# Uneven key blocks, 128-token rows, and keys and queries transposed as float32r words, in an attention and channel-mixing kernel

## The chip, the cores and the metric

The kernel runs on one core of one Trainium2 chip, in one launch. The metric is the device time of an execution in microseconds (us), the median of several; every time below is of the hardware profiler or of these executions.

## The reference, cut to what matters

```python
# q, k, v: (4, 12, 448, 64) float32
scores = (1.0 / np.sqrt(64)) * np.matmul(q, k.transpose(0, 1, 3, 2))
scores = np.where(mask, -1000000000.0, scores)       # causal, 448 x 448
scores = scores - np.max(scores, axis=-1, keepdims=True)
attn = np.exp(scores)
attn = attn / (np.sum(attn, axis=-1, keepdims=True) + 1e-09)
attn_out = np.matmul(attn, v)                        # -> x: (4, 448, 768)
xt = x.transpose(0, 2, 1)                            # token mixing
u = x + (np.maximum(xt @ w_tok1, 0.0) @ w_tok2).transpose(0, 2, 1)
x = u + np.maximum(u @ w_ch1, 0.0) @ w_ch2           # channel mixing
x_prev = shift_by_one_token(x)
xk = mu_k * x + (1.0 - mu_k) * x_prev
xr = mu_r * x + (1.0 - mu_r) * x_prev
k = np.maximum(xk @ w_k, 0.0)
out = 1.0 / (1.0 + np.exp(-(xr @ w_r))) * (k * k @ w_v)
```

Here `w_tok1` is 448 x 256, `w_tok2` 256 x 448, and the weights arrive as 64-bit floats (split64, L275, turns them into pairs of float32r words).

## The kernel before, in words

There are two phases. Phase 0 (to about 345 us of the span) does the attention, the token mixing and the first part of channel mixing; phase 1 does the rest, almost wholly as long float32r matrix products. A product that needs more than float32r's precision is made of three (mm3, L636): high by high, high by low, low by high, each with a weight load and a matmul (L640, L641, L642).

The attention goes by pairs of heads of one batch, 24 pairs (`pair`, L1587), six in each of four batches. One pair does this, with tokens in four chunks of CP = 112:

- `load` (L1595): keys, queries and values come to SBUF as [112, 4, 2, 64] tiles, two DMAs for each (one for each head) on SyncE's (SP's) queue. Only the second head's keys and queries of pair 0 are issued from ScalarE.
- `turn` (L1608): TensorE transposes the four chunks of keys, and the four of queries (L1613), in float32: the chunk [112, 128] is the weights that are loaded, the identity (112 columns) moves through. ScalarE copies the result out as high part; VectorE makes the low part in pairs 6 to 23. Pairs 0 to 5 ("whole", L1593) multiply in plain float32 instead.
- `score` (L1626): queries by keys, causal, query chunk c against the keys of chunks 0 to c. The two heads lie in different halves of the array's rows and run abreast.
- `neg_max` (L1653, with the mask), `expo` (L1671), `recip`, `norm` (L1691): the softmax, on VectorE, ScalarE and GpSimd. The exponentials of query chunk c go to a tile `e` of a rotating pool of four, at `eoff[c]`, 112 x (c + 1) columns wide.
- `et_tr` (L1709): TensorE transposes `e` by blocks of 112 queries by 112 keys (L1716), 20 for each pair; `et_copy` takes them out of PSUM.
- `pv` (L1725): values are the loaded weights (64 columns for each head, two heads abreast in different column halves), and the transposed exponentials move. Key chunk kc moves S - 112 kc columns: 448, 336, 112, 224, in plain float32, which is two matmuls for each head and chunk (L1732).
- `nat` (L1743): TensorE turns the result back to token rows, four transposes of 112 tokens (L1750); `nat_hi` (L1753, ScalarE) and `nat_lo` (L1757, VectorE) write the high and low parts, one instruction each.

Three pairs make a half (384 channels). `tok_half` (L1834) then mixes tokens: `k1` (L1840) multiplies the four token chunks of `w1` by the half, three matmuls for a chunk, for two blocks t of 128 output rows; `k2` (L1872) multiplies by `w2`. There are eight halves. `early_ch1` fills TensorE between these with channel-mixing products (tile `pd`).

The order is not that of the code: `op` (L111) records every step with a due time, an engine, a planned cost, what it reads and writes and which buffers it uses. `walk` (L124) is a list scheduler that then emits all steps in a planned order, one fixed program for each engine. TensorE has three modes in it, "F" (whole array), "R" (score, row halves) and "C" (pv, column halves). MODE (L100) is what the planner adds for a change of mode, STICK how much later a due time may be to stay in the mode. NUDGES (L216) and LATER (L237) are lists of seeds, each of which moves some due times of phase 0 or phase 1 by a pseudo-random amount.

## Time and profile before

| | |
|---|---|
| median of 3 runs | 887.84 us (887.79 to 888.03) |
| the profiled execution | 887.97 us |
| span of its instructions | 886.2 us |
| PE busy | 875.1 us (99% of the span) |
| DVE, ACT, POOL busy | 75%, 59%, 8% |
| granted TensorE clock, mean | 1.00 of full |
| DMA | 164.30 MB, 185 GB/s |

The profile is of one execution. Engines are PE (TensorE matmul), PEld (TensorE weight load, beside PE), DVE (VectorE), ACT (ScalarE), POOL (GpSimd), SP (SyncE); an engine's name with a q is its queue of DMA issues and waits. A row of the timeline gives the start, the time that the merged instructions cover, engine, line, operation, what is written and read, shape and count. Matmuls overlap in the records: a matmul's own duration is longer than the step from its start to the next one's, and it is the step that counts for the time.

### The profile page before, as it was taken

The numbers are of one execution on the slowest core, as the hardware profiler recorded it, in microseconds if no ns is written. First come the engines' busy times: TensorE is split into PE (matmuls) and PEld (weight loads), VectorE is DVE, ScalarE is ACT, GpSimd is POOL, SyncE is SP. The second block draws the span as 40 slices with busy tenths as digits, with TensorE's granted clock in tenths as the row PEclk, the third lists the DMA queues.
The fourth block names the chain that finished last, engine by engine and source line by source line (L and its number), as shares of the span: only waits on it lengthen the run. The fifth ranks groups of instructions, "written<-read, shape, count | busy, mean of one in ns | idle before, by whom it ended". The sixth has DMA issues, their size and how long they took to land.

```text
span 886.2 us, 15923 instructions
## 1 busy us (share of the span) xinstructions
PE 875.1 (99%) x5277; PEld 777.4 (88%) x5277; DVE 667.2 (75%) x1638; ACT 523.6 (59%) x1264; POOL 71.6 (8%) x176
## 2 busy tenths in 40 slices
PE   7999999999999999999999999999999999999998
PEld 4678888878887888888899888999999889999997
DVE  6989998775677756887664766859789867888773
ACT  7988978674878654554441444627566667853330
POOL 1322311100220200000000200100000000000000
PEclk9999999999999999999999999999999999999999
DMA  9656665774666432666797784764647644676642
GB/s 188 167 151 160 166 185 153 213 189 133 176 183 182 158 126 85 173 193 198 272 332 264 232 259 142 257 208 149 207 154 247 209 146 131 205 226 209 181 129 80
DMA packets 178161, 164.30 MB, mean 185 GB/s; under 512 B 79840, under 2 KB 157664, under 8 KB 178080
## 3 DMA queue, kind: packets, MB, share of 16 engines
q1 hardware_dynamic: 177152, 163.08, 60.7%
q8 instruction: 41, 0.67, 0.3%
q14 instruction: 40, 0.33, 0.1%
q10 hardware_dynamic: 928, 0.23, 0.1%
HBM read 110.17 MB, written 53.08 MB: 184 GB/s over the span
## 4 chain that ended last, share of the span: by engine, by line
PE 94%; ACT 3%; DVE 1%; DMA 1%; issue 0%; SPq 0%; DVEq 0%; ACTq 0%
PE acc L642 7%; PE acc L641 7%; PE acc L640 7%; PE ph L640 5%; PE ph L641 5%; PE ph L642 5%; PE pe L1716 5%; PE pv L1732 5%; PE pv L640 4%; PE pv L642 4%; PE pv L641 4%; PE pk L640 4%; PE pk L641 4%; PE pk L642 4%; PE ps L1647 4%; PE pd L640 3%
## 5 line engine op out<-in xcount | busy, mean ns | idle before, releaser
L1675 ACT ACTIVATE e<-ms,nm 112x448 f32<-112x448 f32 (+3 forms) x192 | 100.4, 528 | 11.3 <-DVE nm L1659 10.3
L642 PE MATMUL acc<-a,w 128*128 128x512 f32 (+1 forms) x288 | 104.2, 362 | 0.0
L641 PE MATMUL acc<-a,w 128*128 128x512 f32 (+1 forms) x288 | 104.2, 362 | 0.0
L640 PE MATMUL acc<-a,w 128*128 128x512 f32 (+1 forms) x288 | 104.1, 362 | 0.0
L1659 DVE CUSTOM_DVE_ANT_0 ms<-ps,mask 112x112 f32<-112x112 f32 (+3 forms) x192 | 76.5, 440 | 19.0 <-PE ps L1647 16.2
L1693 POOL TENSOR_SCALAR e<-e,rc 112x336 f32<-112x336 f32 (+3 forms) x100 | 51.9, 537 | 220.1 <-DVE rc L1689 158.8
L642 PE MATMUL pv<-wv,kk 128*128 128x384 f32 x196 | 65.5, 334 | 0.0
L640 PE MATMUL pv<-wv,kk 128*128 128x384 f32 x196 | 65.5, 334 | 0.0
L641 PE MATMUL pv<-wv,kk 128*128 128x384 f32 x196 | 65.5, 334 | 0.0
L263 ACT COPY et<-pe 112x448 f32<-112x448 f32 x102 | 49.4, 538 | 25.3 <-PE pe L1716 24.9
L642 PE MATMUL pk<-a,wk 128*128 128x512 f32 (+1 forms) x168 | 60.8, 362 | 0.0
L641 PE MATMUL pk<-a,wk 128*128 128x512 f32 (+1 forms) x168 | 60.8, 362 | 0.0
L640 PE MATMUL pk<-a,wk 128*128 128x512 f32 (+1 forms) x168 | 60.7, 362 | 0.0
L640 PEld LDWEIGHTS acc<-a,w 128*128 128x128 f32 x288 | 54.1, 188 | 5.6
L641 PEld LDWEIGHTS acc<-a,w 128*128 128x128 f32 x288 | 54.1, 188 | 5.6
L642 PEld LDWEIGHTS acc<-a,w 128*128 128x128 f32 x288 | 54.1, 188 | 5.6
L429 ACT CAST kk<-a 128x512 fp32r<-128x512 f32 x49 | 29.9, 621 | 48.2 <-PE pv L642 37.1
L1716 PE MATMUL pe<-ident,e 112*112 112x112 f32 x480 | 57.2, 261 | 0.8 <-DVE et L263 0.5
L1716 PEld LDWEIGHTS pe<-ident,e 112*112 112x112 f32 x480 | 48.9, 133 | 9.6 <-issue 2.7
L640 PE MATMUL pd<-a,w 128*128 128x384 f32 (+1 forms) x144 | 55.9, 388 | 0.0
L640 PE MATMUL ph<-a,w 128*128 128x512 f32 (+1 forms) x144 | 53.5, 372 | 0.0
L642 PE MATMUL ph<-a,w 128*128 128x512 f32 (+1 forms) x144 | 53.5, 371 | 0.0
(156 smaller groups left out, 2277.4 us busy)
## 6 DMA issues: line engine op xcount, KB each, us to landing
raw<-in_moe_w_ch_dram SPq DMA_DIRECT2D x48, 384.0 KB, 3.4
a<-a_d SPq DMA_DIRECT2D x28, 256.0 KB, 5.0
raw<-in_moe_w_k_dram SPq DMA_DIRECT2D x16, 384.0 KB, 4.2
raw<-in_moe_w_v_dram SPq DMA_DIRECT2D x16, 384.0 KB, 4.8
x_d<-t SPq DMA_DIRECT2D x24, 256.0 KB, 3.5
a<-x_d SPq DMA_DIRECT2D x24, 256.0 KB, 5.4
vn<-in_v_dram SPq DMA_DIRECT2D x48, 112.0 KB, 3.0
s_d<-tmp SPq DMA_DIRECT2D x28, 192.0 KB, 3.9
```

What stands on the lines that cost most here:

```text
L263: nc.scalar.copy(o, i) if by == ACT else nc.vector.tensor_copy(o, i)
L429: nc.scalar.copy(dest()[0], src())
L640: nc.tensor.matmul(o, lh, rh, start=start and i == 0, stop=False, skip_group_check=skip)
L641: nc.tensor.matmul(o, lh, rl, start=False, stop=False, skip_group_check=skip)
L642: nc.tensor.matmul(o, ll, rh, start=False, stop=stop and i == n - 1, skip_group_check=skip)
L1647: nc.tensor.matmul(T["s", j, c], T["q"][r, x, qc], T["k"][r, y, :n], start=i == 0, stop=i == 2,)
L1659: nc.vector.tensor_tensor_reduce(out=ms[:, :n], in0=T["s", j, c], in1=mask[:, S - n:], scale=-0.125, scalar=BIG, op0=ALU.add, op1=ALU.min, ...
L1675: nc.scalar.activation(T["e", j][:, eoff[c]:eoff[c + 1]], T["ms", j, c][:, :n], AF.Exp, bias=T["nm"][:, j, c:c + 1], scale=-1.0, accum_out ...
L1693: (nc.gpsimd if by == POOL else nc.vector).tensor_scalar(out=ec, in0=ec, scalar1=T["rc"][:, j, c:c + 1], scalar2=1.0, op0=ALU.mult, op1=AL ...
L1716: nc.tensor.transpose(pe[:CP, o + (c - kc) * CP:o + (c - kc + 1) * CP], T["e", j][:, eoff[c] + kc * CP:eoff[c] + (kc + 1) * CP], ident[:CP ...
L1732: nc.tensor.matmul(T["pv"][64 * j:64 * j + 64, kc * CP:S], T["vn"][:, kc, j, :], T["et"][:, o:o + S - kc * CP], start=kc == 0, stop=kc == 2,)
```

## The change

- Keys are cut into blocks of 128, 128, 120 and 72 (KEYS) where the exponentials are transposed and multiplied by the values; queries stay in 112s. `e` becomes 1272 columns wide, four fixed buffers, with the unused columns of each chunk set to zero once, by 16 memsets on GpSimd. Values are loaded by four DMAs instead of two.
- Token rows after the attention are cut into 128, 128, 128 and 64. The last chunk of `xh` holds the high part of its 64 tokens in rows 0 to 63 and the low part in rows 64 to 127; the last chunk of `w1` holds the high part twice, so that two matmuls do what three did. `nat_hi` and `nat_lo` become two instructions each.
- For pairs 6 to 23 keys and queries are copied from the inputs to a DRAM tensor `q_d` of the kernel (`keep`, a DMA from DRAM to DRAM, two for each pair, planned 40 us ahead of the pair and after the transposes of four pairs before it), loaded from there into float32r tiles and transposed as float32r against a float32r identity, which ScalarE copies once.
- The planner's MODE goes from 0.1 to 0.18 and STICK from 1.5 to 3.0; about 100 seeds are added to NUDGES, and LATER is another list. PAIR, FILL and the due times of the steps are the same.

```diff
...
-    eoff = [CP * c * (c + 1) // 2 for c in range(NCH + 1)]
+    KEYS = (0, 128, 256, 376, S)
+    KN = [KEYS[c + 1] - KEYS[c] for c in range(NCH)]
+    ew = [KEYS[c] + 128 for c in range(NCH)]
+    eoff = [sum(ew[:c]) for c in range(NCH + 1)]
...
-    ident = cpool.tile([128, 128], F32, name="ident")
-    make_identity(nc, ident)
+    one = wraw.tile([128, 384], F32, tag="tmp", name="one")[:, :128]
+    make_identity(nc, one)
+    identr = cpool.tile([128, 128], F32R, name="identr")
+    nc.scalar.copy(identr, one)
+    ident = identr.bitcast(F32)
...
+    q_d = dpool.tile([2, NP * B, 2, S, D], F32, name="q_d")
...
-    MODE, STICK, WAIT = 0.1, 1.5, 0.08
+    MODE, STICK, WAIT = 0.18, 3.0, 0.08
...
-    LATER = (8900003, 8900009, 8900010, 8900024, 8903014)
+    LATER = (8900009, 8900010, 8900011, 8900024, 8900074, 8900085, 8900150, 8900282)
...
-    def split64(t, key, use, dest, src, pp, n, blocks=False, lead=0):
+    def split64(t, key, use, dest, src, pp, n, blocks=False, lead=0, twice=False):
...
+            if twice:
+                for rows in (slice(0, pp // 2), slice(pp // 2, pp)):
+                    nc.sync.dma_start(dst[rows], src)
+                return
...
         def low(by=DVE):
...
-            (nc.gpsimd if by == POOL else nc.vector).tensor_sub(lo, box["tmp"], hi.bitcast(F32))
+            rows = slice(0, pp // 2 if twice else pp)
+            (nc.gpsimd if by == POOL else nc.vector).tensor_sub(
+                lo, box["tmp"][rows], hi[rows].bitcast(F32)
+            )
...
+    KEPT = NP
     def tp(g):
...
-        ep = c0.enter_context(tc.tile_pool(name="ep", bufs=4))
+        ep = c0.enter_context(tc.tile_pool(name="ep", bufs=1))
...
+        ebufs = [ep.tile([CP, eoff[NCH]], F32, name=f"e{i}") for i in range(4)]
+        for x in ebufs:
+            for c in range(NCH):
+                nc.gpsimd.memset(x[:, eoff[c] + (c + 1) * CP:eoff[c + 1]], 0.0)
+        etaken = []
...
-        w1 = tw.tile([CP, 2, NCH, DT], F32R, name="w1")
+        w1 = tw.tile([128, 2, NCH, DT], F32R, name="w1")
+        nc.gpsimd.memset(w1[64:, 1, NCH - 1, :].bitcast(F32), 0.0)
...
         def tok_weights(t0, dt, early):
...
-                pp = t.shape[0]
-                src = w.rearrange("(c p) (a n) w -> c a p n w", p=pp, n=n)
...
+                    rows = slice(128 * c, min(128 * c + 128, w.shape[0]))
+                    lows = rows.stop - rows.start
...
-                            lambda t=t, c=c, cs=cs: (t[:, 0, c, cs], t[:, 1, c, cs]),
-                            src[c, i], pp, n, lead=10 if t0 < early else 0,
+                            lambda t=t, c=c, cs=cs, lows=lows: (t[:, 0, c, cs], t[:lows, 1, c, cs]),
+                            w[rows, cs], 128, n, lead=10 if t0 < early else 0, twice=lows < 128,
...
             def load(nm, src):
...
-                    [CP, NCH, 2, D], F32, tag=f"{nm}n", name=f"{nm}n", bufs=3 if nm == "v" else 2
-                )
+                    [128 if nm == "v" else CP, NCH, 2, D], F32R if nm != "v" and g >= KEPT else F32,
+                    tag=f"{nm}n", name=f"{nm}n",
+                    bufs=3 if nm == "v" else 2,
+                )
+                if nm == "v":
+                    for j in range(2):
+                        nc.sync.dma_start(
+                            nat[:, :2, j, :],
+                            src[b, 2 * p + j, :KEYS[2]].rearrange("(c p) d -> p c d", p=128),
+                        )
+                    for c in (2, 3):
+                        nc.sync.dma_start(
+                            nat[:KN[c], c],
+                            src[b, 2 * p:2 * p + 2, KEYS[c]:KEYS[c + 1]].rearrange("j p d -> p j d"),
+                        )
+                    return
...
+                    if g >= KEPT:
+                        nc.sync.dma_start(
+                            nat[:, :, j, :].bitcast(F32),
+                            q_d["kq".index(nm), g, j].rearrange("(c p) d -> p c d", p=CP),
+                        )
+                        continue
...
+            def keep(i, src):
+                nc.sync.dma_start(q_d[i, g], src[b, 2 * p:2 * p + 2])
             def turn(nm):
...
-                    nc.tensor.transpose(pt[:, c * CP:(c + 1) * CP], x, ident[:CP, :CP])
+                    o = pt[:, c * CP:(c + 1) * CP]
+                    if g >= KEPT:
+                        nc.tensor.transpose(o.bitcast(F32R), x, identr[:CP, :CP])
+                    else:
+                        nc.tensor.transpose(o, x, ident[:CP, :CP])
...
             def expo(j, c):
...
-                    T["e", j] = ep.tile([CP, eoff[NCH]], F32, tag="e", name="e")
+                    T["e", j] = ebufs[len(etaken) % len(ebufs)]
+                    etaken.append((g, j))
...
-                    T["e", j][:, eoff[c]:eoff[c + 1]],
+                    T["e", j][:, eoff[c]:eoff[c] + n],
...
 -                ec = T["e", j][:, eoff[c]:eoff[c + 1]]
+                ec = T["e", j][:, eoff[c]:eoff[c] + (c + 1) * CP]
...
             def et_tr(i):
...
-                    T["et"] = etp.tile([CP, len(groups) * S], F32, tag="et", name="et")
+                    T["et"] = etp.tile([128, len(groups) * S], F32, tag="et", name="et")
...
-                            pe[:CP, o + (c - kc) * CP:o + (c - kc + 1) * CP],
-                            T["e", j][:, eoff[c] + kc * CP:eoff[c] + (kc + 1) * CP],
+                            pe[:, o + (c - kc) * CP:o + (c - kc + 1) * CP],
+                            T["e", j][:, eoff[c] + KEYS[kc]:eoff[c] + KEYS[kc] + 128],
...
             def pv():
...
-                        o = place[j, kc]
+                        o = place[j, kc] - kc * CP
...
-                            T["pv"][64 * j:64 * j + 64, kc * CP:S],
-                            T["vn"][:, kc, j, :],
-                            T["et"][:, o:o + S - kc * CP],
+                            T["pv"][64 * j:64 * j + 64, KEYS[kc]:S],
+                            T["vn"][:KN[kc], kc, j, :],
+                            T["et"][:KN[kc], o + KEYS[kc]:o + S],
...
             def nat():
...
-                    hv["xh"] = xp.tile([CP, 2, NCH, 3, 128], F32R, tag="xh", name="xh")
+                    xh = xp.tile([128, 7, 3, 128], F32R, tag="xh", name="xh")
+                    hv["xh"] = [xh[:, :3], xh[:, 3:6]], xh[:, 6]
...
-                    nc.tensor.transpose(pnr[:CP, c, :], T["xT"][:, c * CP:(c + 1) * CP], ident)
+                    x = T["xT"][:, c * 128:min(c * 128 + 128, S)]
+                    nc.tensor.transpose(pnr[:x.shape[1], c, :], x, ident)
...
             def nat_hi():
-                hv = halves[b, p // 3]
-                nc.scalar.copy(hv["xh"][:, 0, :, i3, :], T["nat"][:CP])
+                (hi, _), last = halves[b, p // 3]["xh"]
+                nc.scalar.copy(hi[:, :, i3, :], T["nat"][:, :3])
+                nc.scalar.copy(last[:64, i3, :], T["nat"][:64, 3])
...
             def nat_lo():
-                xh = halves[b, p // 3]["xh"]
+                (hi, lo), last = halves[b, p // 3]["xh"]
+                nc.vector.tensor_sub(lo[:, :, i3, :], T["nat"][:, :3], hi[:, :, i3, :].bitcast(F32))
...
-                    xh[:, 1, :, i3, :], T["nat"][:CP], xh[:, 0, :, i3, :].bitcast(F32)
+                    last[64:, i3, :], T["nat"][:64, 3], last[:64, i3, :].bitcast(F32)
...
+                kept = []
+                if nm != "v" and g >= KEPT:
+                    kept = [(nm + "d", g)]
+                    keeps.append((s0 - 40, keep, i, src, kept))
...
-                    w=[(nm + "n", g)], u=[(nm + "n", g)],
+                    r=kept, w=[(nm + "n", g)], u=[(nm + "n", g)],
...
-                s0 + 16, PE, 2.1, pv, r=[("et", i, g) for i in range(5)] + [("vn", g)], w=[("pv", g)],
+                s0 + 16, PE, 1.86, pv, r=[("et", i, g) for i in range(5)] + [("vn", g)], w=[("pv", g)],
...
-            op(s0 + 16.5 - EV, ACT, 0.465, nat_hi, r=[("pn", g)], w=[("xhi", g)], u=u)
-            op(s0 + 16.5 - EV, DVE, 0.6, nat_lo, r=[("xhi", g)], w=[("xlo", g)], u=u)
+            op(s0 + 16.5 - EV, ACT, 0.56, nat_hi, r=[("pn", g)], w=[("xhi", g)], u=u)
+            op(s0 + 16.5 - EV, DVE, 0.68, nat_lo, r=[("xhi", g)], w=[("xlo", g)], u=u)
...
-                xh = hv["xh"]
+                (hi, lo), last = hv["xh"]
...
+                o = hv["ph", t][:, :HALF]
+                if c < NCH - 1:
+                    x = [y[:, c].rearrange("p a m -> p (a m)") for y in (hi, lo)]
+                    mm3(o, [((w1[:, 0, c, ts], w1[:, 1, c, ts]), x)], start=c == 0, stop=False)
+                    return
+                x = last.rearrange("p a m -> p (a m)")
+                nc.tensor.matmul(o, w1[:, 0, c, ts], x, start=False, stop=False)
+                nc.tensor.matmul(o, w1[:, 1, c, ts], x, start=False, stop=True)
...
-                        s1 + 0.1 * c, PE, 0.53, k1, t, c,
+                        s1 + 0.1 * c, PE, 0.53 if c < NCH - 1 else 0.35, k1, t, c,
...
+        for t, f, i, src, key in keeps:
+            op(t, SP, dma(2 * S * D * 4), f, i, src, r=[("pt", "q", key[0][1] - 4)], w=key)
...
```

## Rows read from the trace of the kernel before

**Rows 1.** Busy time by stretch: from:to, length, PE, PEld, DVE, ACT, POOL, clock, DMA, GB/s.
```profile
0.00:45.00 45.00, 38.65 (x269) 25.31 (x269) 35.47 (x144) 39.11 (x121) 10.39 (x27) 1.00 0.83 175
45.00:100.00 55.00, 54.98 (x433) 44.21 (x432) 49.58 (x161) 48.78 (x144) 15.60 (x26) 1.00 0.64 171
...
250.00:345.00 95.00, 94.67 (x666) 82.03 (x665) 62.93 (x188) 57.69 (x158) 10.97 (x24) 1.00 0.48 151
```

**Rows 2.** The chain that ended last, around 13 us: start us, us, what.
```profile
12.70 0.38 SPq L1602
...
13.13 3.98 DMA kn<-in_k_dram
```

**Rows 3.** Timeline around 185 us, weight loads: transposes of queries, then float32r products.
```profile
184.71 0.43 PEld L1613 LDWEIGHTS pt<-ident,qn 112*128 112x128 f32 x4
...
185.09 0.19 PEld L640 LDWEIGHTS pd<-a,w 128*128 128x128 f32 x1
...
185.20 0.19 PEld L641 LDWEIGHTS pd<-a,w 128*128 128x128 f32 x1
```

**Rows 4.** Timeline of PEld at 184.4 us: the first load alone, and the first two together.
```profile
184.36 0.14 PEld L1613 LDWEIGHTS pt<-ident,kn 112*128 112x128 f32 x1 [0.32 <-issue]
...
184.36 0.20 PEld L1613 LDWEIGHTS pt<-ident,kn 112*128 112x128 f32 x2 [0.32 <-issue]
```

**Rows 5.** PEld of score at 196 us (112 columns), and ns of such loads, min/median/max.
```profile
196.04 0.47 PEld L1647 LDWEIGHTS ps<-kt,qt 64*112 64x112 f32 x8
...
L1647 PEld LDWEIGHTS ps<-kt,qt x114: 169/172/175, 67.4 to 117.5; 64*112 64x112 f32 x114
```

**Rows 6.** Groups by form, pv: count, busy us and mean ns of one.
```profile
L1732 PE MATMUL pv<-et,vn 112*64 112x336 f32 x96 | 17.6, 446 | 0.0
...
L1732 PE MATMUL pv<-et,vn 112*64 112x224 f32 x96 | 13.2, 352 | 0.0
```

**Rows 7.** Timeline of PE at 331 us: k1, float32r, 384 columns.
```profile
331.12 0.33 PE L640 MATMUL ph<-xh,w 112*128 112x384 f32 x1
331.29 0.33 PE L641 MATMUL ph<-xh,w 112*128 112x384 f32 x1
331.47 0.33 PE L642 MATMUL ph<-xh,w 112*128 112x384 f32 x1
```

**Rows 8.** Timeline of PE at 195 us: long products, then score, then pv.
```profile
194.93 0.39 PE L641 MATMUL pd<-a,w 128*128 128x512 f32 x1
195.16 0.39 PE L642 MATMUL pd<-a,w 128*128 128x512 f32 x1
195.48 1.32 PE L1647 MATMUL ps<-kt,qt 64*112 64x336 f32 x18
196.73 2.11 PE L1732 MATMUL pv<-et,vn 112*64 112x448 f32 x16
```

**Rows 9.** Timeline, the first 9 us.
```profile
0.73 0.43 ACTq L1602 DMA_DIRECT2D kn<-in_k_dram  x1
...
1.66 0.28 POOL L1561 TENSOR_SCALAR_AFFINE_SELECT mask<-mask 112x112 f32<-112x112 f32 x1
...
1.78 1.28 ACT L1606 ACT_TABLE_LOAD   x1 [1.78 <-issue]
...
4.00 0.42 PE L1613 MATMUL pt<-ident,kn 112*128 112x112 f32 x1 [4.00 <-DMA kn<-in_k_dram]
...
9.01 0.28 DVE L1659 CUSTOM_DVE_ANT_0 ms<-ps,mask 112x112 f32<-112x112 f32 x1
```

**Rows 10.** Groups by form of ACT: exponentials, the widest and the narrowest.
```profile
L1675 ACT ACTIVATE e<-ms,nm 112x448 f32<-112x448 f32 x48 | 32.0, 669 | 4.1 <-DVE nm L1659 3.2 <-POOL e L1693 0.8
...
L1675 ACT ACTIVATE e<-ms,nm 112x112 f32<-112x112 f32 x48 | 18.5, 386 | 1.4 <-DVE nm L1659 1.4
```

**Rows 11.** SP's issues of values (ns, min/median/max); DMAs to u_d (KB, us to landing).
```profile
L1602 SPq DMA_DIRECT2D vn<-in_v_dram x48: 312/482/1424, 2.7 to 288.5; - x48
...
u_d<-xT SPq DMA_DIRECT2D x18, 224.0 KB, 3.5
```

More of the change, by code (lines that the diff above doesn't have):

```diff
@@ L1691, in norm @@
             def norm(j, c, by):
-                ec = T["e", j][:, eoff[c]:eoff[c + 1]]
+                ec = T["e", j][:, eoff[c]:eoff[c] + (c + 1) * CP]
                 (nc.gpsimd if by == POOL else nc.vector).tensor_scalar(
@@ L1722, in et_copy @@
             def et_copy(i, by):
-                copy_by(by, T["et"][:, S * i:S * (i + 1)], T["pe", i][:CP, :S])
+                copy_by(by, T["et"][:, S * i:S * (i + 1)], T["pe", i][:, :S])
             def pv():
@@ L1844, in k1 @@
                     hv["ph", t] = ps_m.tile([128, 512], F32, tag="m", name="ph")
-                xh = hv["xh"]
+                (hi, lo), last = hv["xh"]
                 ts = slice(t * 128, (t + 1) * 128)
-                mm3(
-                    hv["ph", t][:, :HALF],
-                    [
-                        (
-                            (w1[:, 0, c, ts], w1[:, 1, c, ts]),
-                            (
-                                xh[:, 0, c].rearrange("p a m -> p (a m)"),
-                                xh[:, 1, c].rearrange("p a m -> p (a m)"),
-                            ),
-                        )
-                    ],
-                    start=c == 0,
-                    stop=c == NCH - 1,
-                )
+                o = hv["ph", t][:, :HALF]
[6 more added lines that the diff above has]
+                nc.tensor.matmul(o, w1[:, 1, c, ts], x, start=False, stop=True)
             def k1_hi(t):
@@ L2003, in early_ch1 @@
                 op(t + 7, SP, dma(128 * W * 4), store, j, r=[("er", b, j)], w=[("h_d", b, j)], u=[h])
+        keeps = []
         GATE, LOW = 10, 60
```

13 rows, old and new, of the table NUDGES are left out of this document.

## The prediction

> **What bounds the kernel now.** I read the stretches first [rows 1]. From 45 us on TensorE is busy without a gap: 54.98 of 55 us, and still 94.67 of 95 us at the end of phase 0. There a microsecond of TensorE work taken away is a microsecond of time, as long as the others keep up: VectorE is at 49.58 of 55 us (90%) early and at 62.93 of 95 us (66%) late. The first 45 us are different: TensorE has 38.65 us, ScalarE 39.11 us, the DMA engines are 83% busy, and the chain of waits there runs over a load of keys, 3.98 us from SP's issue to landing [rows 2]. So the change is read twice: TensorE's work after 45 us, and the other engines' work and the queue before.
>
> **The change part by part.** The sum is made against the profiled execution (887.97 us, which is its span of 886.2 us and 1.8 us around it).
>
> *Float32r transposes.* Pairs 6 to 23 have 18 x 8 = 144 of them. Now four loads and the matmuls behind them take 185.09 - 184.71 = 0.38 us, 0.096 us each [rows 3]. Two things can set the new step. One is the columns: float32r takes 0.175 us for 384 columns [rows 7] and 0.23 for 512 [rows 8], so 0.43 ns for a column, and 0.175 - 272 x 0.00043 = 0.058 us for 112. The other is the load of 128 columns, and here the trace has two kinds. In the transposes, before the matmuls hold it back, the second load follows the first by 0.20 - 0.14 = 0.06 us [rows 4]. In float32r products it follows by 0.11 us [rows 3]; score's float32r loads of 112 columns go four pairs in 0.47 us, the last lasting 0.17, so 0.10 us a pair [rows 5]. The chunk is now a float32r word, but in a transpose. I take 0.06 us: the row with the same line, tile shape and purpose is the nearest. 144 x (0.096 - 0.060) = -5.2 us. The ends: 0.048 us (112 columns with no fixed part), -6.9 us; 0.11 us, +2.0 us.
>
> The Trainium skill, page "TensorE: Matmul & The Clock Gate", section "LDWEIGHTS (loading the stationary operand)", gives a load as its columns divided by 1.2 a nanosecond, whatever the type: an estimate of 0.107 us for 128. The float32r loads of this trace agree with it (0.11), the float32 loads of the transposes do not (0.06). By it this part would be +1.6 us instead of -5.2.
>
> *Values.* The columns moved for a head fall from 448 + 336 + 224 + 112 = 1120 to 448 + 320 + 192 + 72 = 1032. 112 columns less make a pv matmul 446 - 352 = 94 ns shorter [rows 6], 0.84 ns a column. All 16 of a pair take about 2.1 us [rows 8], half of 4 x 1120 x 0.84 ns = 3.8 us, so the two heads run abreast and two passes count: 88 x 2 x 0.84 = 0.148 us a pair. In the 21 pairs after the first 45 us: -3.1 us.
>
> *Token mixing.* Eleven matmuls in place of twelve, for 2 blocks in 8 halves: 16 x 0.175 us [rows 7] = -2.8 us.
>
> *The other transposes.* Twenty of `e` in each pair now load 128 columns instead of 112 and move as many as before; the 128-column loads of the same type fit into 0.096 us [rows 3, 4]. `nat` moves 128 identity columns as before. Nothing for both; what hides the longer load is the two-pass matmul beside it.
>
> *Order.* Going from long products to score costs 195.48 - 195.16 = 0.32 us where the step is 0.23 [rows 8], 0.09 us, and the way back is taken as the same. STICK at twice its value saves some of these. With one block of score fewer in every fourth pair and three such drains to a block (in, start, out), 6 x 0.27 = 1.6; I take -1.0. Ends: 0, and one block fewer in each pair, -6.5. A new order can as well lose in places what the old one had: +2 is the other end. LATER touches only phase 1, where TensorE has no gaps to give: 0, within 0.5 either way.
>
> *The start.* ScalarE's copy of the identity stands ahead of its two DMA issues. Now ScalarE issues the second head's keys at 0.73; in future it may first load its table (1.28 us) and copy 128 columns, some 0.4 us by the exponentials [rows 9, 10]. Then the first transposes at 4.00 us move by up to 1.6 us; if the 16 memsets (some 2 us at 0.13 each, an estimate from the 0.28 us of a 112 x 112 select) go ahead of the identity on GpSimd, by 2.4. Nothing, if the issue stays first. I take +1.2. The mask, done at 1.94 now and perhaps 4.4 then, is needed at 9.01 [rows 9].
>
> *Split instructions.* On ScalarE an instruction has a fixed part: 669 ns for 448 columns, 386 for 112 [rows 10], 0.84 a column, so 0.29 us fixed. One more `nat_hi` and, as an estimate alike, `nat_lo` in each pair: hidden behind TensorE later, 4 pairs x 0.2 us = +0.8 us before 45 us (0 to 1.5).
>
> *The queue.* Two more issues of values are 2 x 0.48 us of SP for a pair [rows 11]; three such pairs are loaded in the first 25 us, where loads are waited for [rows 2]. +0.5 us (0 to 2.9). The 36 copies in DRAM (224 KB each, as one u_d store, which lands in 3.5 us [rows 11]) issue in 17 us of SP over 300 and are planned 28 us ahead of the load behind them. Their 8.3 MB, counted once or as read and written, add 16 to 32% to the 51 MB that 171 GB/s make in 300 us, at which the DMA engines are 64% busy or less [rows 1]. Hidden: 0. If that cover is gone, the second rival gives the price.
>
> Sum: -5.2 - 3.1 - 2.8 - 1.0 + 1.2 + 0.8 + 0.5 = -9.6, so 878.4 us against 887.97, and with the median 0.1 us below that execution (887.84), **878.2 us**.
>
> **The rivals.**
> *1. The float32r load sets the step.* At 0.11 us a transpose the part costs +2.0 instead of -5.2: 878.2 + 7.2 = 885.4 us. For it: every float32r load in the trace takes that pace, at 112 and at 128 columns. Against it: none of these is a transpose. The page named above would have it so too.
>
> *2. The copies hold up the loads (the slower side).* The copy of a pair waits on SP for the transposes of four pairs before it, everything behind it in the queue waits along, and the loads of keys and queries wait for its landing. SP's queue is in order, so a copy that comes to its head too early delays the loads of the pairs before. It decides when keys or queries come later than TensorE's other work lasts; 18 pairs that lose 0.8 us each are 14.4, and -9.6 + 14.4 gives 892.6 us. For it: 83% busy DMA at the start and a chain over a load. Against: from 45 us on not one such wait shows, and there is 28 us of lead.
>
> *3. VectorE becomes the bound up to 150 us.* It is at 90% there and gets `nat_lo`'s second instruction. Then the gains up to 150 us, some 7 of 18 pairs of transposes (1.9) and as much of the rest (2.0), go into waits: 882.1 us. For it: 90%. Against: the weight conversions on VectorE have due times far ahead and can move.
>
> **How the numbers follow.** The forecast (0.55) gives 878.2, and its own terms reach from about 872 to 883. Rival 1 (0.23): 885.4; rival 3 (0.15): 882.1; rival 2 (0.07): 892.6. With 1 in 10 left out on each side the range is 872 to 886. A measurement of this kernel can tell 0.2% (1.8 us) from no change: under 886.1 is faster. Forecast and rival 3 lie there almost wholly, rival 1 in two cases of three: 0.55 + 0.14 + 0.15 = 0.84 faster. The rest of rival 1 is no change, 0.08, and rival 2 with a little of the others slower, 0.08.
>
> **What would show it.** In the profile after: L1613's line for pairs 6 on with four transposes in 0.24 us (right), 0.44 (rival 1) or 0.38 (nothing gained); pv at about 1.9 us for 16 instead of 2.1; 176 matmuls of k1 instead of 192; first transposes at 5.2 instead of 4.0; no wait of PE on `kn` or `qn` after 45 us (against rival 2), VectorE under 95% from 45 to 150 us (against rival 3). The prediction is wrong if phase 0 ends less than 7 us earlier, or if phase 1, from its first `acc` matmul to its end, changes by more than 1 us.

## The result, and the profile after

The changed kernel takes **892.75 us** (median of 4 runs, 891.52 to 893.77), the kernel before beside it 887.93: ratio 1.0052, interval 1.0040 to 1.0065. It is slower. 878.2 was forecast, and the second rival's 892.6 lies beside what came. The profiled execution took 893.65 us, its span is 891.9.

First the page's part 1 (busy us, share, instructions) and the stretches of [rows 1] (same columns) in the changed kernel:

```profile
PE 872.7 (98%) x5261; PEld 772.2 (87%) x5261; DVE 681.8 (76%) x1679; ACT 527.6 (59%) x1285; POOL 67.2 (8%) x180
```
```profile
0.00:45.00 45.00, 36.28 (x242) 22.62 (x244) 34.21 (x137) 35.97 (x114) 12.14 (x41) 0.96 0.78 191
45.00:100.00 55.00, 52.14 (x407) 40.92 (x405) 52.28 (x164) 45.11 (x135) 14.82 (x24) 1.00 0.71 198
100.00:150.00 50.00, 48.51 (x381) 41.43 (x377) 44.96 (x142) 38.48 (x110) 8.78 (x14) 1.00 0.64 184
150.00:200.00 50.00, 48.43 (x354) 40.78 (x355) 42.89 (x131) 38.72 (x106) 2.70 (x5) 1.00 0.78 227
```

The last two stretches in the kernel before:

```profile
100.00:150.00 50.00, 49.88 (x376) 43.84 (x375) 45.21 (x138) 39.94 (x110) 9.76 (x17) 1.00 0.61 168
150.00:200.00 50.00, 50.00 (x379) 40.95 (x377) 36.62 (x117) 36.44 (x99) 5.35 (x11) 1.00 0.65 182
```

Against these and [rows 1] TensorE now has gaps where it had almost none: 2.86 us between 45 and 100 us, 1.5 us in each of the next two stretches. VectorE rose from 49.58 to 52.28 of 55 us, and the chain of waits says who sets the end in 45 to 100 us, first before, then in the changed kernel (the rows end where the view cuts them):

```profile
by line: PE pv L1732 18.6%; PE pe L1716 16.9%; PE ps L1647 14.3%; PE pt L1613 6.7%; PE ph L640 5.9%; PE ph L642 5.1%; PE ph L641 5.1%; PE pn L1750 4.7%; PE pu L640 4.5%; PE pu L642 4.4%; PE pu L641 4.4%; PE ps L1638 3.4%; PE pd L641 2.4%; P
```
```profile
by line: DVE ms L1722 18.6%; DVE e L1757 12.5%; PE pv L1796 10.2%; DMA a<-u_d 6.6%; PE pe L1780 5.4%; DVE et L283 4.1%; issue 3.7%; DVE h L1934 3.5%; DVE xh L1827 3.4%; DVE qt L1684 3.1%; DVE xT L1953 2.8%; PE pu L667 2.8%; DVE kt L1684 2.7
```

Before, all of this chain was TensorE's. Now VectorE has 35.7 us of it, above all with maxima (`ms`), divisions (`e`) and evictions, and TensorE 13.2.

The timelines that answer to [rows 9] (first transposes) and to the end of phase 0 (first `acc` matmul, in the changed kernel and then in the kernel before):

```profile
4.01 0.98 PE L1676 MATMUL pt<-identr,kn 112*128 112x112 f32 x4 [4.01 <-DMA kn<-in_k_dram]
...
352.85 0.39 PE L667 MATMUL acc<-a,w 128*128 128x512 f32 x1
```
```profile
347.43 0.39 PE L640 MATMUL acc<-a,w 128*128 128x512 f32 x1
```

The start is where it was (4.00). Phase 1 began at 347.43 us and begins at 352.85, 5.4 us later; from there to the last matmul it takes what it took (534.2 us before, 534.4 now). So nearly all of it happens in phase 0.

The work itself changed as forecast. Groups by form, pv from 58.7 to 231 us (to be read against [rows 6]), and the weight loads of float32r transposes near 255 us (against [rows 3]):

```profile
L1796 PE MATMUL pv<-et,vn 128*64 128x320 f32 x52 | 9.2, 432 | 0.0
L1796 PE MATMUL pv<-et,vn 120*64 120x192 f32 x52 | 6.4, 325 | 0.0
```
```profile
254.55 0.42 PEld L1674 LDWEIGHTS pt<-identr,qn 112*128 112x128 f32 x4
254.92 0.41 PEld L1674 LDWEIGHTS pt<-identr,kn 112*128 112x128 f32 x4
255.27 0.19 PEld L667 LDWEIGHTS pd<-a,w 128*128 128x128 f32 x1
```

The two forms are 14 and 27 ns shorter than the 446 and 352 they replace. Four float32r transposes take 0.35 to 0.37 us where four float32 ones took 0.38.

Two chains show where the new transfers stand. The first is around 20 us (L1658 loads keys and queries, L1665 issues a copy), with the clock of that time from the stretches (same columns as above):

```profile
20.54 0.55 SPq L1665
...
21.14 1.37 SPq L1665
...
22.61 0.53 SPq L1658
...
23.18 3.57 DMA qn<-in_q_dram
```
```profile
24.00:27.00 3.00, 1.59 (x13) 1.20 (x13) 3.00 (x13) 2.73 (x9) 1.80 (x4) 1.00 0.85 185
27.00:30.00 3.00, 3.00 (x13) 1.55 (x13) 1.48 (x7) 2.07 (x7) 0.00 (x0) 0.59 0.96 274
30.00:35.00 5.00, 4.82 (x41) 3.36 (x41) 4.72 (x17) 4.07 (x14) 1.48 (x3) 0.91 0.86 222
```

Two copies stand 1.92 us in SP's queue ahead of queries that TensorE waits for. It is idle for 1.41 us of 24 to 27, and then the granted clock is 0.59 and 0.91, most of 3 us at the lower level of 1.2 GHz: an estimate of 3 x 0.41 + 5 x 0.09 = 1.7 us more. Between 150 and 200 us a weight load (L311) stands behind seven issues of the same queue, 3.9 us in all, of which one is a copy (L1665, 0.49 us):

```profile
187.83 0.49 SPq L1665
188.38 0.58 SPq L1652
...
191.69 0.02 SPq L311
191.74 5.04 DMA raw<-in_moe_w_ch_dram
```

### The profile page after: what moved, and what is told of

Same layout as the page of the kernel before. It is cut to its first block, busy times and chain, and to the rows that moved or that the text cites. A ratio compares the mean times of both kernels' runs of the same rounds, so it can differ in the third digit from the quotient of the medians.

```text
span 891.9 us, 16047 instructions
## 1 busy us (share of the span) xinstructions
PE 872.7 (98%) x5261; PEld 772.2 (87%) x5261; DVE 681.8 (76%) x1679; ACT 527.6 (59%) x1285; POOL 67.2 (8%) x180
## 4 chain that ended last, share of the span: by engine, by line
PE 85%; DVE 7%; DMA 3%; ACT 3%; issue 1%; SPq 1%; DVEq 0%; ACTq 0%
PE acc L669 6%; PE acc L667 6%; PE acc L668 6%; PE ph L667 4%; PE ph L669 4%; PE ph L668 4%; PE pe L1780 4%; PE pv L668 4%; PE pv L669 4%; PE pv L667 4%; PE pk L668 4%; PE pk L669 4%; PE pk L667 4%; PE pv L1796 3%; PE pr L668 3%; PE pr L669 3%
## 5 line engine op out<-in xcount | busy, mean ns | idle before, releaser
L1739 ACT ACTIVATE e<-ms,nm 112x112 f32<-112x112 f32 (+3 forms) x192 | 100.3, 526 | 18.2 <-DVE nm L1722 17.9
L1722 DVE CUSTOM_DVE_ANT_0 ms<-ps,mask 112x448 f32<-112x448 f32 (+3 forms) x192 | 76.4, 443 | 17.5 <-PE ps L1710 15.3
L1780 PE MATMUL pe<-identr,e 112*128 112x112 f32 x480 | 59.2, 264 | 3.8 <-DVE xh L1828 2.0
L1780 PEld LDWEIGHTS pe<-identr,e 112*128 112x128 f32 x480 | 50.9, 143 | 12.9 <-issue 3.4
L1757 POOL TENSOR_SCALAR e<-e,rc 112x336 f32<-112x336 f32 (+3 forms) x82 | 43.3, 546 | 216.5 <-DVE rc L1753 135.8
L283 ACT COPY et<-pe 128x448 f32<-128x448 f32 x95 | 46.7, 537 | 17.3 <-PE pe L1780 17.0
```

Of the source, the lines that this page charges most:

```text
L283: nc.scalar.copy(o, i) if by == ACT else nc.vector.tensor_copy(o, i)
L1722: nc.vector.tensor_tensor_reduce(out=ms[:, :n], in0=T["s", j, c], in1=mask[:, S - n:], scale=-0.125, scalar=BIG, op0=ALU.add, op1=ALU.min, ...
L1739: nc.scalar.activation(T["e", j][:, eoff[c]:eoff[c] + n], T["ms", j, c][:, :n], AF.Exp, bias=T["nm"][:, j, c:c + 1], scale=-1.0, accum_out ...
L1757: (nc.gpsimd if by == POOL else nc.vector).tensor_scalar(out=ec, in0=ec, scalar1=T["rc"][:, j, c:c + 1], scalar2=1.0, op0=ALU.mult, op1=AL ...
L1780: nc.tensor.transpose(pe[:, o + (c - kc) * CP:o + (c - kc + 1) * CP], T["e", j][:, eoff[c] + KEYS[kc]:eoff[c] + KEYS[kc] + 128], ident[:CP ...
```

## The experiments

Three theories stood at first: the order that new seeds and settings give, the copies, and that other engines take up TensorE's saving. In what follows "before's order" means that every engine gets its instructions in the order of the kernel before. "Part one" is the key blocks and token rows without part two (copies and float32r words).

**Parts of the change under the planner.** The first kernel keeps the changed kernel's order and takes the copies, their loads and float32r away; the second takes part two away in the planner too, so that it orders anew; the third and fourth exchange the settings and the lists of seeds. A line `...` marks what is left out.

```diff
# same_order_no_copy: after
...
-                nc.sync.dma_start(q_d[i, g], src[b, 2 * p:2 * p + 2])
+                pass
...
-                        nc.tensor.transpose(o.bitcast(F32R), x, identr[:CP, :CP])
+                        nc.tensor.transpose(o, x, ident[:CP, :CP])
# no_part_two: after
-    KEPT = NP
+    KEPT = NP * B
# old_settings: after (before_new_settings: before, the other way round)
-    MODE, STICK, WAIT = 0.18, 3.0, 0.08
+    MODE, STICK, WAIT = 0.1, 1.5, 0.08
...
```

> The changed kernel with its instruction order kept, but without the copies in DRAM: keys and queries of pairs 6 to 23 are loaded from the inputs and transposed as float32; the planner still counts the copies. Theory A (the copies and what they do to SP's queue and the DMA engines cost the time): 884 us or less, the stalls of TensorE before 345 us fall by over 8 us. Theory B (the planned order costs the time, wherever the words come from): 892 to 895 us; the transposes cost some 144 x 0.011 = 1.6 us more than as float32r, and the stalls stay.

> The changed kernel with the keys' and queries' part left out, order planned anew without the copies. Theory A: 884 us or less. Theory B, if the seeds fit the program with its copies or fit neither: anything, but by the order; if the seeds were made for the program without the copies: 880 us or less, with the order as the reason.

> The changed kernel with MODE, STICK, NUDGES and LATER of the kernel before. Theory A: 891 to 894 us, as changed. Theory B: another order, so another time by several us, either way; below 888 us if the added seeds are what costs it.

> The kernel before with MODE, STICK, NUDGES and LATER of the changed one. Theory A: within 2 us of 888. Theory B: slower than 888 by 5 us or more, as seeds chosen for another program are as good as random ones for this one.

Measured: 889.59 us (ratio 1.0019, 1.0009 to 1.0028); 913.97 (1.0292, 1.0277 to 1.0308); 907.66 (1.0223, 1.0208 to 1.0238); 917.34 (1.0332, 1.0316 to 1.0348). A setting or a set of seeds used on a program that it was not found for costs up to 29 us. So orders of the planner can't be compared part by part. The first of these kernels, with 5.9 us less TensorE work than before, is still 1.7 us slower than it; that lies between what theory A (884 or less) and theory B (892 to 895) asked for.

**Parts of the change in before's order.** That takes the planner out of the comparison.

```diff
# old_order_part_one: after, with before's settings, seeds and costs
...
-                        nc.tensor.transpose(o.bitcast(F32R), x, identr[:CP, :CP])
+                        nc.tensor.transpose(o, x, ident[:CP, :CP])
# old_order_part_one_copies: old_order_part_one (old_order_both: the copies also loaded, float32r)
+                if nm == "k" and KEPT <= nxt < NP * B:
...
+                        nc.sync.dma_start(q_d[i2, nxt], s2[b2, 2 * p2:2 * p2 + 2])
# copies_but_float32: after
...
-                        nc.tensor.transpose(o.bitcast(F32R), x, identr[:CP, :CP])
+                        nc.tensor.transpose(o, x, ident[:CP, :CP])
# old_order_token_rows: old_order_part_one
-    KEYS = (0, 128, 256, 376, S)
+    KEYS = (0, 112, 224, 336, S)
...
```

> The order of the kernel before on every engine, instruction for instruction, with the key blocks and token rows of the change and without its keys' and queries' part. If the order costs the time and the shorter pv and token mixing are worth what their steps say (3.1 + 2.8 us): 881 to 883 us. If the split instructions, the four value loads and the start cost as much as is saved, whatever the order: 887 us or more.

> As old_order_part_one, and the 36 copies in DRAM issued two pairs ahead, just before the load of keys, without use. If the copies disturb the loads by themselves (SP's queue, DMA engines): 3 us or more above old_order_part_one. If they are hidden: within 1 us of it.

> As old_order_part_one_copies, and the copies are loaded and transposed as float32r words. Against that run the faster transposes should give 144 x 0.011 = 1.6 us. If the change's parts are good and its order is what costs: 880 to 884 us.

> The changed kernel in its own order, copies made and loaded, but the transposes as float32. Against the changed kernel (892.75): 1.6 us slower, 894.4, if the faster transposes show on the path; the same, if TensorE waits for others anyway. Against the same order without copies (889.59) the difference is what the copies cost alone, 3 to 5 us by the first two results.

> The order of the kernel before and its key blocks of 112, so values are loaded by two DMAs as before; of the change only the token rows in 128s (eleven matmuls for twelve, split instructions). If the two more issues for each pair's values on SP's queue are what ate the gain of old_order_part_one (887.25 instead of 882): 885 us, the 2.8 us of k1 shown. If the split instructions ate it, or TensorE's work was never what set the time: 887 to 888.5 us.

Measured: part one 887.25 us (0.9992, 0.9983 to 1.0002); with copies that nobody reads 894.06 (1.0069, 1.0054 to 1.0084); with copies used and float32r 892.58 (1.0056, 1.0040 to 1.0073); the changed kernel with float32 transposes 891.78 (1.0041, 1.0026 to 1.0056); token rows alone 887.07 (0.9987, 0.9978 to 0.9996).

So the copies cost 6.8 us in before's order and 2.2 in the changed kernel's (889.59 to 891.78). In before's order pair 1's first value matmul comes 4.4 us later than with part one alone; in the chain of waits ahead of it stand the loads beside the first copies:

```profile
20.84 3.96 DMA small<-in_moe_mu_r_dram
...
26.42 3.65 DMA raw<-in_moe_w_tok_dram
```

Another 2.4 us go near 240 us, where the chain stands 4.57 us on a load of queries: pair 16's values are 4.0 us late (235.7 instead of 231.7), pair 17's 6.4 (250.4 instead of 244.0). And up to 1.7 of the 6.8 us (2 x 0.09 + 2 x 0.50 + 2 x 0.26, an estimate) are the clock, which falls here and stays at 1.00 with part one alone:

```profile
32.00:34.00 2.00, 1.98 (x15) 1.50 (x15) 2.00 (x10) 2.00 (x7) 0.00 (x0) 0.91 0.78 213
34.00:36.00 2.00, 2.00 (x11) 1.29 (x10) 1.97 (x9) 2.00 (x8) 0.31 (x1) 0.50 0.98 242
36.00:38.00 2.00, 2.00 (x18) 0.82 (x14) 1.04 (x7) 2.00 (x9) 2.00 (x6) 0.74 0.86 282
```

In the changed kernel's order the runs don't show where the 2.2 us lie. With float32 transposes pair 1's values begin at 30.3 us with the copies and at 30.2 without; in the changed kernel's profile, with the stall at 24 to 27 us, at 32.3. The second copy's issue ahead of that stall took 1.37 us there and 0.59 in copies_but_float32, whose profiled execution is its fastest (890.51 us).

Float32r transposes seem to give 1.5 us in before's order, but the intervals overlap, and of the 1.1 us between the two profiles 0.7 are there at pair 3's values (62.3 against 63.0 us), behind the clock's fall in one of them. They give nothing in the changed kernel: of its four runs the two with a mean clock of 0.998 took 893.65 and 893.77 us, those with 0.999 and 1.0 took 891.52 and 891.85, as much as copies_but_float32. And part one brings 0.6 us, with an interval that holds no change, where 5.9 us of TensorE work went. Token rows alone, with two value loads as before, bring about 1 of 2.8 us, so the two more value issues of a pair are not all that eats the saving. In part one's stretches TensorE is idle where it wasn't before:

```profile
45.00:100.00 55.00, 53.66 (x425) 43.01 (x424) 49.64 (x163) 48.72 (x147) 15.58 (x26) 1.00 0.62 170
100.00:150.00 50.00, 48.46 (x364) 42.16 (x363) 46.02 (x142) 38.79 (x112) 9.68 (x17) 1.00 0.62 168
```

**Another queue, or fewer copies.**

```diff
# part_one_values_pool: old_order_part_one, the last two loads of values
-                        nc.sync.dma_start(
+                        nc.gpsimd.dma_start(
...
# old_order_both_pool: old_order_both, the copies
-                        nc.sync.dma_start(q_d[i2, nxt], s2[b2, 2 * p2:2 * p2 + 2])
+                        nc.gpsimd.dma_start(q_d[i2, nxt], s2[b2, 2 * p2:2 * p2 + 2])
# old_order_both_late: old_order_both
-    KEPT = NP
+    KEPT = NP + 5
```

> As old_order_part_one, but the last two of a pair's four value loads are issued from GpSimd's queue, so that SP issues as many as before. If SP's queue ate the gain: 883 to 885 us. If not: 887 us, or more where GpSimd's own work delays the values.

> As old_order_both (892.58), but the copies in DRAM are issued from GpSimd's queue. If it is SP's queue that the copies clog: 886 to 888 us. If it is the DMA engines that they occupy (packets of 14 KB, 0.72 us each, between others of 256 B): as old_order_both, 891 to 894 us.

> As old_order_both, but only pairs 11 to 23 are copied and transposed as float32r, the first copy some 45 us later. If the copies cost only where the start waits for its loads: 886.5 us (old_order_part_one less 13 x 8 x 0.011 = 1.1 us), plus what the one late stall near 240 us costs, up to 2.3 us. If they cost everywhere alike: 890 us.

Measured: 888.71 us (1.0012, 1.0002 to 1.0021); 902.31 (1.0167, 1.0146 to 1.0189); 890.26 (1.0024, 1.0015 to 1.0034). GpSimd is the worse place: in the chain of the second an issue of 0.53 us stands at 235.54 us ahead of three divisions (2.07 us), and a weight load takes 7.58 us. Leaving the copies of pairs 6 to 10 away spares 2.3 us, but what is left costs more than part one alone.

**Where part one's saving goes.** Two suspects are taken away one at a time: VectorE's work (the clamp in each of 52 weight conversions of phase 0 is left out, so words out of range are not limited there) and the doubled value loads in SP's queue.

```diff
# light_before, light_part_one, light_after
         def clamp():
+            if state.get("emit", 0) == 0:
+                return
# three_value_loads: old_order_part_one (light_three_value_loads: light_part_one)
-                            nat[:, :2, j, :],
-                            src[b, 2 * p + j, :KEYS[2]].rearrange("(c p) d -> p c d", p=128),
+                            nat[:, :3, j, :],
+                            src[b, 2 * p + j, :384].rearrange("(c p) d -> p c d", p=128),
-                    for c in (2, 3):
-                        nc.sync.dma_start(
-                            nat[:KN[c], c],
-                            src[b, 2 * p:2 * p + 2, KEYS[c]:KEYS[c + 1]].rearrange("j p d -> p j d"),
-                        )
+                    nc.sync.dma_start(
+                        nat[:KN[3], 3],
+                        src[b, 2 * p:2 * p + 2, KEYS[3]:].rearrange("j p d -> p j d"),
+                    )
# retuned_part_one: no_part_two, with seeds searched for it
-    MODE, STICK, WAIT = 0.18, 3.0, 0.08
+    MODE, STICK, WAIT = 0.1, 1.5, 0.08
...
```

> The kernel before with the clamp of each weight conversion of phase 0 left out (52 VectorE instructions of about 0.34 us, 17.5 us of VectorE; the words themselves are still converted), every other instruction in the same order. Before's chain in 45 to 150 us is over 93% TensorE, so all theories expect little here: 885 to 888 us. If VectorE's queue already sets the step in the kernel before, 880 to 884.

> Before's order with key blocks and token rows and no copies (887.25 us), with the same 52 clamps left out. Theory V (TensorE's saved 5.9 us were turned into waits because VectorE's queue of maxima, divisions and evictions runs only just behind it): with 18 us of VectorE gone the saving comes through, 4 to 6 us below the kernel before with the same clamps left out. Theory O (the waits come from an order written for other durations, on all engines): within 1.5 us of the kernel before with the clamps left out. Theory W (the transfers of weights and values set it): within 1.5 us as well, with DMA and SP in the chain of 45 to 150 us.

> The changed kernel (892.75 us) with the same clamps of phase 0 left out. Theory V: 885 to 888 us, phase 1 beginning 5 to 7 us earlier than at 352.85. Theory W: 890 to 893 us, the chain between 150 and 200 us still with DMA at 30% or so. Theory O: 890 to 893 us.

> Key blocks and token rows without copies, float32 loads and transposes, with seeds and settings of the planner searched for this program and its durations (the switch of TensorE's mode charged 0.1 and 1.5 us), so every engine's order is new. Theory O: 880 to 884 us, the 5.9 us that key blocks and token rows take off TensorE come through and phase 1 begins at 340 to 343 us. Theory V or W: 886 to 890 us, since VectorE and the transfers have as much to do as before.

> Before's order with key blocks and token rows and no copies (887.25 us), but the values of a pair come in three loads instead of four: the first three blocks of 128 rows by head (8 rows more than are used), then the last 72 rows of both heads. 24 SP issues of some 0.45 us fewer, nothing else. If SP's queue of value loads, ahead of the third edge load at 63.61 us and of the values near 96 us, is part of where the saving went: 886.3 to 886.9 us, the third edge load issued 0.4 to 0.5 us earlier. If not: 887.0 to 887.5 us.

> The same three value loads with the 52 clamps of phase 0 left out as well (885.1 us with four loads). If VectorE's queue and SP's issues each hold back a share of their own: 884.0 to 884.7 us. If SP's issues are hidden: 885.0 to 885.3 us. Nothing under 883.5 us is expected, since the chain ahead of 45 us is ScalarE's, where less TensorE work gives nothing.

Measured: light_before 887.48 us (0.9996, 0.9987 to 1.0006); light_part_one 885.10 (0.9971, 0.9959 to 0.9983); light_after 890.08 (1.0024, 1.0013 to 1.0034); retuned_part_one 888.82 (1.0009, 0.9999 to 1.0018); **three_value_loads 885.62 (0.9970, 0.9959 to 0.9980)**; light_three_value_loads 885.23 (0.9964, 0.9952 to 0.9977).

An order searched for part one did not help: the 880 to 884 us that theory O asked for did not come, though one search doesn't rule out a better order. A stretch at a clock of 0.68 and 0.75 from 18 to 24 us costs it 1.7 us, but even its runs at full clock took 887.94 and 888.02. Leaving out the 52 clamps takes 14 us off VectorE's busy time (671.6 to 657.2 in part one). It gives nothing in the kernel before, 2.1 us in part one and 2.7 in the changed kernel; of the latter up to 1.7 can be the clock, which in its profile stays at 1.00 from 27 to 35 us. The 2.4 us between light_part_one and light_before lie between what theory V (4 to 6) and theories O and W (1.5 at most) asked for. Three value loads give 1.6 us, more than expected. Both together give no more than the lighter VectorE alone: they relieve the same wait, and the trace shows one. SP's queue near 120 us, first before, then part one, then three loads (`raw` is a weight block for channel mixing):

```profile
119.50 0.38 SPq L287 DMA_DIRECT2D raw<-in_moe_w_ch_dram  x1
```
```profile
118.77 1.13 SPq L1628 DMA_DIRECT2D vn<-in_v_dram  x2
119.96 0.97 SPq L1633 DMA_DIRECT2D vn<-in_v_dram  x2
121.04 0.39 SPq L300 DMA_DIRECT2D raw<-in_moe_w_ch_dram  x1
```
```profile
119.59 0.45 SPq L1632 DMA_DIRECT2D vn<-in_v_dram  x1
120.15 0.37 SPq L300 DMA_DIRECT2D raw<-in_moe_w_ch_dram  x1
```

The values of two pairs stand ahead of the weights. With eight issues instead of four the block is asked for 1.54 us later than before, with six 0.65 us later. In part one it lands at 124.46 us, and its conversion then meets GpSimd's subtraction of another block. VectorE's and GpSimd's timeline of part one, with the clamp (L312) twice, and the same rows with three loads:

```profile
123.67 0.35 DVE L312 TENSOR_SCALAR tmp<-tmp 128x384 f32<-128x384 f32 x1
...
125.99 1.21 DVE L312 TENSOR_SCALAR tmp<-tmp 128x384 f32<-128x384 f32 x1
...
131.03 1.14 DVE L1932 TENSOR_TENSOR xT<-pu,xT 128x448 f32<-128x448 f32 x2
```
```profile
125.97 1.01 POOL L335 TENSOR_TENSOR w<-tmp,w 128x384 fp32r<-128x384 f32 x1 [3.83 <-ACT w L330]
```
```profile
125.35 0.35 DVE L312 TENSOR_SCALAR tmp<-tmp 128x384 f32<-128x384 f32 x1
...
129.53 1.14 DVE L1931 TENSOR_TENSOR xT<-pu,xT 128x448 f32<-128x448 f32 x2
```
```profile
125.34 1.23 POOL L335 TENSOR_TENSOR w<-tmp,w 128x384 fp32r<-128x384 f32 x1 [3.48 <-ACT w L330]
```

Behind GpSimd's subtraction the clamp takes 1.21 us instead of 0.35, and the eviction that TensorE waits for (`xT`) begins at 131.03 instead of 129.53. The Trainium skill, page "SBUF — State Buffer", section "SBUF: two separate sides", says that GpSimd and VectorE, the latter in a two-port mode or with two inputs in SBUF, hold one pair of ports by an exclusive lock, and that the loser waits for the other's whole instruction. These rows agree (1.21 us behind an instruction of 1.01); the clamp's mode no run here shows.

The values of pair 10, and then the first `acc` matmul at the end of phase 0, begin so in part one, with three loads and in light_part_one (before, it is 136.22 and 347.43 us):

```profile
137.85 0.97 PE L1776 MATMUL pv<-et,vn 128*64 128x448 f32 x4
...
346.92 0.39 PE L656 MATMUL acc<-a,w 128*128 128x512 f32 x1
```
```profile
136.34 1.51 PE L1775 MATMUL pv<-et,vn 128*64 128x448 f32 x8
...
345.10 0.39 PE L656 MATMUL acc<-a,w 128*128 128x512 f32 x1
```
```profile
135.96 1.80 PE L1781 MATMUL pv<-et,vn 128*64 128x448 f32 x14
...
344.56 0.39 PE L661 MATMUL acc<-a,w 128*128 128x512 f32 x1
```

Between the two, the three versions gain 2.1, 2.4 and 2.6 us on the kernel before, of some 3.7 us of work taken away there (14 pairs x 0.14, ten matmuls of k1 x 0.175). Ahead of it they gain 0.3 us at most. One place where the saving may end stands in the chain of all three: the third load `a<-u_d`, behind the values in SP's queue, and ScalarE's cast of it. In part one, and then before:

```profile
66.82 0.51 ACT L734 CAST a<-a 128x384 fp32r<-128x384 f32 x1 [0.91 <-DMA a<-u_d]
```
```profile
66.42 0.51 ACT L718 CAST a<-a 128x384 fp32r<-128x384 f32 x1
```

With three loads the cast begins at 66.62 us, in light_part_one at 66.42: never earlier than before, though TensorE has less to do. What was taken from VectorE lies mostly elsewhere: between 45 and 100 us it fell from 49.64 to 47.99 us only.

## Why the prediction was wrong

- *"There a microsecond of TensorE work taken away is a microsecond of time, as long as the others keep up."* This step failed, and with it the two terms that were sized rightly. Values and token mixing shrank as the working said: in part one six pairs from 58.7 us on have 11.27 us of pv steps instead of 12.13, so 0.14 us a pair less where 0.148 was said, and there are 176 matmuls of k1 instead of 192. Yet 5.9 us less work gave 0.6 us less time, and the changed kernel took longer. The TensorE without a gap in [rows 1] said only that TensorE was never the one to wait. It didn't say how close behind the others were. Up to 115 us nothing came through. After 136 us more than half did (2.1 to 2.6 of 3.7 us).
- *Queue of values, +0.5 (0 to 2.9).* Misplaced, though its range holds what came: three loads instead of four give 1.6 us back, not in the first 25 us but most of it by one weight block that came late near 124 us.
- *Copies, hidden, 0.* Wrong: +2.2 us in the changed kernel's order, +6.8 in before's, there with up to 1.7 of clock. In before's order their issues stand in a queue that delivers just in time, and the loss sits in two spots, before pair 1's values and near 240 us. 64% busy DMA engines told nothing of that. Rival 2 had the mechanism, but that its time is 0.2 us off is luck: it put 14.4 us on the copies, 0.8 on each of 18 pairs, and they cost 2.2.
- *Float32r transposes, -5.2.* Mis-sized: the step is about 0.088 us (0.35 / 4), neither 0.060 nor 0.11, so 144 x (0.096 - 0.088) = 1.2 us of TensorE. Rows 4 showed the first two loads of a group, after the loads had paused for 0.32 us; that was no rate, as all four with the matmuls behind them take 0.38 in rows 3. The Trainium skill's page "TensorE: Matmul & The Clock Gate", section "LDWEIGHTS (loading the stationary operand)", would have given an estimate of 0.107 us; the trace agrees neither with it nor with the 0.060 of the prediction. What the 1.2 us are worth in time the runs don't show.
- *Order, -1.0.* Wrong sign: the changed kernel's order without copies, 889.59, against before's order with the same work, 887.25, is +2.3 us. One thing in it can be seen: the divisions of `e` done by GpSimd fell from 100 to 82, so 18 more are VectorE's, which already had 90%. That they are the cause was not tested.
- *The start, +1.2.* Nothing: 4.01 us. ScalarE's DMA issues were not delayed.
- *Split instructions, +0.8.* Not separated. They are part of the VectorE load that light_part_one lightens.
- *Rival 3* named the engine that the changed kernel's chain has from 45 to 100 us. No run shows that VectorE costs the time there: light_part_one's 2.1 us come mostly between 115 and 136 us, and light_after's gain past the clock, 1.0 us or more, was not located. Its cost adds to rival 2's and doesn't stand against it. *LATER* was right at 0.

The sum, from 887.9 us: part one -0.6, its order +2.3, copies +2.2, float32r transposes with the clock's fall +1.0, each a difference of two kernels above, ends at 892.75. What stays open is what holds part one back ahead of 115 us: there neither fewer loads nor a VectorE lighter by 1.7 us gave anything, and ScalarE, with 48.72 of 55 us, was not lightened. Open too are the cause of the order's 2.3 us and the place of the copies' 2.2.

## What to carry to other kernels

An engine that is busy without a gap sets the time only as far as the next engine and the queues behind it have slack; before costing its savings in full, look at what would be waited for if it were 1% faster, stretch by stretch. In a queue served in order, count what a new issue pushes back, most of all the loads that land just in time; here one more value load in each pair took back 1.6 of the 5.9 us. The version to keep is part one in before's order with three value loads: 885.62 us, faster than both kernels.

## What the runs showed of the hardware that was not expected

- Float32r transposes of 112 x 128 follow each other in 0.088 us, float32 ones in 0.096; neither the load nor the columns alone give that.
- A VectorE clamp of 128 x 384 took 1.21 us instead of 0.35 behind a GpSimd subtraction; where both began together (three value loads) the clamp took 0.35 and the subtraction 1.23 instead of 1.01.
- A TensorE pause of 1.13 us for queries in one piece, 1.41 us in 3, was followed by a granted clock of 0.59 over the next 3 us. A longer one in old_order_both, 2.13 us in one piece, was not: the granted clock is 1.00 from 27 to 40 us there.
- Copies in DRAM that no one reads cost 6.8 us in before's order, up to 1.7 of it by a clock that fell; issued from GpSimd, with the copies used, the kernel takes 902.31 us instead of 892.58.
